# Tiny softmax steps on ScalarE, a second level for product P1, and the sums of the softmax's product on VectorE: a fused attention and ELU kernel on one core

## The chip, the core and the metric

One core of a Trainium2 chip runs the whole kernel. The metric is the device time of one execution in microseconds (us); the time given for a kernel is the median of its runs.

## What is computed

A block-recurrent cross attention is followed by a feed-forward layer with ELU. All data are float32.

```
x: 8 batches, 8 heads, 512 rows, 64;   state: 8, 8, 32, 64
scores  = x @ state^T / 8;   a  = softmax(scores);    xread = a @ state
scores2 = state @ x^T / 8;   a2 = softmax(scores2);   sread = a2 @ x
X = concat(xread, sread) as (4352 rows, 512)       # 544 rows a batch
h = X @ w_in (512 x 2048);   g = h if h > 0 else exp(h) - 1
out = g @ w_out (2048 x 512)
```

Each softmax subtracts its row's maximum and divides by its row's sum plus 1e-9.

## The kernel before

The rows of `xread` (512 a batch) are handled batch by batch; the 32 rows of `sread` of all batches are collected and handled at the end in `states()`. `a @ state @ w_in` is regrouped: for each batch M = state @ w_in is computed (`make_m`), and the first feed-forward product multiplies the softmax `a` (in the buffer `aT`) by M.

Both large products are done by Strassen-Winograd's scheme, in which sums of blocks are formed first and seven products of half size take the place of eight. For the first product the sums of the softmax's blocks are formed by `sum_a` (four subtractions of 128x256 elements), those of M's blocks by `sum_m`, both on GpSimd. For the second product (`ffn2`, class `Strassen`) there are seven products P1 to P7. P2 to P7 are split once more by the same scheme (class `Second`, the "second level"): `weights` forms sums of the weights once, in batch 1, writing one of them over a block of `w_out`; `sums` forms sums of `g` for every batch on VectorE (up to four of 128x512); `steps` gives seven steps, each of four matmuls with 128 columns and one result of 128x128, which VectorE adds to the output buffer `o` from PSUM, or ScalarE copies where the place is fresh. `restore` undoes the overwritten weights for `states()`. P1 (`a11` times `b11`) is not split: 16 matmuls with 256 columns, and one copy of 128x512 by ScalarE.

The softmax of the next batch lies within `ffn2` (`soft_next`): `softmax` for the one that feeds `aT` (transposes, maxima, sums, GpSimd subtracts and multiplies) and `softmax_rows` for the other, which gives `sread`. Three of their steps are tiny `tensor_scalar` instructions on VectorE: the row maximum times minus the scale (128x2), and the 1e-9 added to the sums (128x2 and 128x32).

Nothing is issued in the order in which it is written. Each call records an operation with an estimated cost; `Plan.order` (called at the end) works out due times backwards from TensorE's order and lists the operations engine by engine, GpSimd in the written order. `plan.behind(op)` keeps what is recorded inside it behind the operation `op`; in `soft_next` that is `late[6]`, the last sum of P7's. An operation with `port` set is not planned beside another one that uses the port of VectorE and GpSimd. Since all instructions are issued by one helper, the profile gives them line 464; they are told apart by their buffers: `small` (statistics of the softmax), `xr` (softmax of batches 2 to 7), `s`, `sec` and `m` (sums), `o` (output and next input), `g` (ELU's result), `ps` (PSUM), `w_half` (`make_m`), `xe` (Exp of ELU, and x).

Of the kernel before, what the change touches and what calls it, by code (L numbers as in the profile page):

```python
# [16 lines left out]
AF = mybir.ActivationFunctionType  # L17
ALU = mybir.AluOpType
# [371 lines left out]
def kernel(  # L390
# [21 lines left out]
    scale = 1.0 / math.sqrt(D)  # L412
    eps = 1e-9
# [16 lines left out]
    plan = Plan(psum)  # L430
# [38 lines left out]
    def is_ap(v):  # L469
        return isinstance(v, (View, bass.AP))  # L470

    class Engine:
# [3 lines left out]
        def __getattr__(self, name):  # L476
            def call(**kw):
                outs = [kw[k] for k in ("out", "accum_out") if k in kw]
                ins = [v for k, v in kw.items() if k not in ("out", "accum_out") and is_ap(v)]
                n = max(elements(a) for a in outs + ins) / 1000  # L480
                wide = [a for a in ins if not isinstance(a, View) and elements(a) > 4]
                port = False
                if self.key == DVE:
                    cost = 0.07 + 1.042 * n
                    alone = len(wide) == 1 and not isinstance(kw["out"], View)
                    if alone and name in ("tensor_scalar", "tensor_copy"):
                        cost, port = 0.07 + 0.53 * n, True
                    port = port or len(wide) > 1
                elif self.key == ACT:
                    cost = 0.055 + 0.84 * n  # L490
                    cost += 0.1 * sum(k in kw and is_ap(kw[k]) for k in ("scale", "bias") if k in kw)
                    cost += 0.1 * ("accum_out" in kw)
                else:
                    cost = 0.06 + (1.86 if name == "tensor_tensor" and n > 0.3 else 2.45) * n
                    port = True
                plan.add(
                    self.key, cost, issue(self.engine, name, kw), ins, outs, port,
                    name=name,
                )

            return call

    V, A, Q = Engine(DVE, nc.vector), Engine(ACT, nc.scalar), Engine(POOL, nc.gpsimd)
# [211 lines left out]
    def sum_a():  # L715

        r11, r12, r21, r22 = a_blocks_of(a_sb)
        t1, t2, t4 = (a_sb[:, 1024 + 256 * i : 1280 + 256 * i] for i in range(3))
        (V if 0 else Q).tensor_tensor(out=t1, in0=r12, in1=r11, op=ALU.subtract)
        (V if 0 else Q).tensor_tensor(out=t2, in0=r22, in1=t1, op=ALU.subtract)  # L720
        (V if 0 else Q).tensor_tensor(out=r12, in0=r22, in1=r12, op=ALU.subtract)
        (V if 0 else Q).tensor_tensor(out=t4, in0=r21, in1=t2, op=ALU.subtract)

    def a_blocks_of(a):
        return [a[:, g * 512 + j * 256 : g * 512 + (j + 1) * 256] for g in range(2) for j in range(2)]
# [8 lines left out]
    def read(b, late=False):  # L734
        return kT[:, (b - 1) % (B + 1)] if b != 1 or not late else read_1

    def softmax_rows(b):
        s = st[b, "s"]
        top, total = small(b)[:, 0:2], small(b)[:, 2:4]
        for g in range(G):  # L740
            V.reduce_max(out=tops(b, g)["top"], in_=s[g], axis=AX_X)
        V.tensor_scalar(out=top, in0=top, scalar1=-scale, scalar2=None, op0=ALU.mult)
        for g in range(G):
            A.activation(
                out=soft_a(b, g), in_=s[g], func=AF.Exp, scale=scale, bias=tops(b, g)["top"],
                accum_out=tops(b, g)["total"],
            )
        V.tensor_scalar(out=total, in0=total, scalar1=eps, scalar2=None, op0=ALU.add)
        V.reciprocal(out=total, in_=total)

    def softmax(b, to):
        s = st[b, "s"]
        total_t = small(b)[:, 36:68]

        def rows(g):
            return soft_t(b, g).rearrange("p (k n) -> p k n", n=NS)

        for g in range(G):
            V.transpose(out=soft_t(b, g), in_=s[g])
        for g in range(G):  # L760
            V.reduce_max(out=tops(b, g)["top_t"], in_=rows(g), axis=AX_X)
            (V if 0 & 1 and b > 1 or b in [] else Q).tensor_tensor(
                out=rows(g), in0=rows(g), in1=bc(tops(b, g)["top_t"], NS), op=ALU.subtract
            )
            A.activation(out=soft_t(b, g), in_=soft_t(b, g), func=AF.Exp, scale=scale)
            V.reduce_sum(out=tops(b, g)["total_t"], in_=rows(g), axis=AX_X)
        V.tensor_scalar(out=total_t, in0=total_t, scalar1=eps, scalar2=None, op0=ALU.add)
        V.reciprocal(out=total_t, in_=total_t)
        for g in range(G):
            (V if 0 & 2 and b > 1 or b in [] else Q).tensor_tensor(  # L770
                out=rows(g), in0=rows(g), in1=bc(tops(b, g)["total_t"], NS), op=ALU.mult
            )
            V.transpose(out=to[:, g * 512 : (g + 1) * 512], in_=soft_t(b, g))
# [149 lines left out]
    b11, b12, b21, b22 = (halves(w_k[:, h, :, e]) for e in range(2) for h in range(2))  # L923
# [8 lines left out]
    class Second:  # L932
# [82 lines left out]
    second = {  # L1015
        k: Second(sec[:, i * 1536 : (i + 1) * 1536]) for i, k in enumerate((7, 5, 4, 3, 6))
    }
# [258 lines left out]
    def ffn2(o, b):  # L1276

        c11, c12, c21, c22 = (o.part(i, j) for i in range(2) for j in range(2))
        nxt = b + 1 < B
        spare = spaces(m_sb[:, 1], 3)  # L1280
        o.sum_1()
        late = [plan.ops[-1]]
        if 0:
            second[1].sums(o.a11, spare + s_2[0][:1])
            steps = second[1].steps(c12, fresh=True)
            steps[0]()
        else:
            x1 = o.open()
            o.product(x1, o.a11, b11, True)
            A.copy(out=c12, in_=x1)  # L1290
            steps = []
        if nxt:
            first_m(b + 1, 1)
            scores(b + 1, xr, [f.view() for f in fixed])
        else:
            turn_read()
        for f in steps[1:]:
            f()
        second[2].sums(o.a12, s_2[1] + spaces(a_sb))
        late.append(plan.ops[-1])  # L1300
        for f in second[2].steps(c11, base=c12):
            f()
        late.append(plan.ops[-1])
        second[4].sums(o.a22, s_2[0] + spare[:2])
        late.append(plan.ops[-1])
        for f in second[4].steps(c21, fresh=True):
            f()
        second[6].sums(o.s, s_2[1] + spaces(a_sb))
        late.append(plan.ops[-1])
        combine(o.a12, o.a12, o.s)  # L1310
        late.append(plan.ops[-1])
        steps = second[6].steps(c12)
        second[7].sums(o.a21, s_2[0])
        late.append(plan.ops[-1])
        for f in steps:
            f()
        combine(o.s, o.s, o.a11, ALU.add)
        late.append(plan.ops[-1])

        def soft_next():  # L1320
            if nxt:
                with plan.behind(late[6]):
                    softmax(b + 1, a_sb)
                    softmax_rows(b + 1)
                    load_x(b + 1, x_halves)
                    move_state(b + 1)
                    sum_a()
                    if 1:
                        sum_m(m_to[0])
        if 1==1: soft_next()  # L1330
        V.tensor_tensor(out=c21, in0=c21, in1=c12, op=ALU.add)
        steps = second[7].steps(c22, fresh=True)
        second[5].sums(o.s, s_2[1])
        late.append(plan.ops[-1])
        if 1==2: soft_next()
        for f in steps:
            f()
        V.tensor_tensor(out=c21, in0=c21, in1=c22, op=ALU.add)
        steps = second[5].steps(c12)
        second[3].sums(o.a12, s_2[0])  # L1340
        for f in steps:
            f()
        V.tensor_tensor(out=c22, in0=c22, in1=c12, op=ALU.add)
        store(b, 1, o)
        steps = second[3].steps(c12)
        if nxt:
            make_m(b + 1, 2, 3)
            copy_m(b + 1, 1, m_to[1])
            sum_m(m_to[1])
            state_read(b + 1)  # L1350
        for f in steps:
            f()
        store(b, 0, o)

    def ffn2_1(o, b, x1):
# [36 lines left out]
            f()  # L1392
        store(b, 1, o)
        second[2].weights(b21)
        if 0: second[1].weights(b11)
        for f in second[3].steps(c12):
            f()
        store(b, 0, o)
# [111 lines left out]
    def states():  # L1510
# [7 lines left out]
        for hc in range(5):  # L1518
            fetch_state(hc)
        for k, i in second.items():  # L1520
            if k > 1 or 0: i.restore()
        xT = st["xT"].rearrange("p m b s -> p m (b s)")
        (r11, r12), (r21, r22) = (
            [xT[:, 2 * k : 2 * k + 2, n * P : (n + 1) * P] for n in range(2)] for k in range(2)
# [1 line left out]
        t1, t2, t4 = (  # L1526
            xr[:, 1024 + i * 256 : 1280 + i * 256].rearrange("p (k n) -> p k n", k=2)
            for i in range(3)
        )
# [93 lines left out]
```

## Time and profile before

| | us |
|---|---|
| median of 3 runs (lowest, highest) | 706.02 (704.77, 706.29) |
| the profiled execution | 707.31 |
| its span, first to last instruction | 705.5 |
| TensorE busy | 692.4 |
| VectorE busy | 577.5 |
| ScalarE busy | 301.3 |
| GpSimd busy | 139.4 |

The page divides the span into 40 slices and gives for each the busy tenth of every engine (PE is TensorE, PEld its weight loads, DVE VectorE, ACT ScalarE, POOL GpSimd). A group's line names engine, operation, out<-in and shape, then the count, the busy time in us, the mean of one in ns, and the idle time of the engine ahead of it with what ended it. Instructions of one engine overlap, so a mean is longer than the distance from one start to the next. A matmul of float32 shows as two records.

### The profile page before, as it was taken

The page shows a single profiled execution, that of the slowest core. Times are in us where ns is not written, and L with a number is a line of the kernel's source. Part 1 is how long each engine was busy: PE and PEld are TensorE (multiplying, and loading weights), DVE is VectorE, ACT ScalarE, POOL GpSimd, SP SyncE. Part 2 cuts the span into 40 slices and gives each one's busy share as a digit, 9 for nine tenths or more (in the row PEclk, how much of TensorE's full clock was granted, in tenths as well). Part 3 has the DMA queues.
Part 4 walks back from the last instruction along what each step waited for, and adds up shares of the span by engine and source line. Part 5 has one row for each costly group of instructions (what it writes and reads, how often), then busy time and mean ns, then how long its engine had stood idle before and what let it go on. Part 6 is the DMA issues. An engine that isn't in the chain of part 4 may idle for free.

```text
span 705.5 us, 14564 instructions
## 1 busy us (share of the span) xinstructions
PE 692.4 (98%) x5802; PEld 591.9 (84%) x5802; DVE 577.5 (82%) x1015; ACT 301.3 (43%) x604; POOL 139.4 (20%) x161
## 2 busy tenths in 40 slices
PE   8899999999999999999999999999999999999997
PEld 7544468889988998889888988899888988899996
DVE  3989999999659895899769995989589976997650
ACT  3999982011157123831275125712383127600530
POOL 1310000042121045101630153103520173000000
PEclk9999999999999999999999999999999999999999
DMA  8677773203261406650283316440575026200300
GB/s 193 208 275 256 265 240 58 60 33 118 91 141 70 120 2 181 149 121 1 60 245 77 70 44 189 98 121 1 153 177 120 2 59 212 62 1 31 120 8 23
DMA packets 111268, 78.55 MB, mean 111 GB/s; under 512 B 89184, under 2 KB 92768, under 8 KB 111200
## 3 DMA queue, kind: packets, MB, share of 16 engines
q1 hardware_dynamic: 108988, 77.06, 38.6%
q8 instruction: 46, 0.75, 0.4%
q10 hardware_dynamic: 2212, 0.56, 0.4%
q14 instruction: 22, 0.18, 0.1%
HBM read 61.34 MB, written 13.11 MB: 106 GB/s over the span
## 4 chain that ended last, share of the span: by engine, by line
PE 82%; DVE 12%; DMA 2%; issue 2%; ACT 1%; SPq 1%; ACTq 0%; DVEq 0%
PE ps L464 82%; DVE small L464 3%; DVE o L464 3%; DVE sec L464 2%; DVE s L464 2%; DMA xe<-in_x_dram 1%; DVE g L464 1%; DMA g<-in_x_dram 1%; SPq L464 1%; DVE xr L464 0%; DVE aT L464 0%; PE ps L1581 0%; ACT sec L464 0%; ACT t_w L464 0%; ACTq L464 0%
## 5 line engine op out<-in xcount | busy, mean ns | idle before, releaser
L464 PE MATMUL ps<-aT,m 128*128 128x256 f32 (+1 forms) x568 | 148.8, 406 | 1.1 <-ACT kT L464 1.1
L464 PE MATMUL ps<-w_out,g 128*128 128x128 f32 (+1 forms) x864 | 144.5, 315 | 0.0
L464 PEld LDWEIGHTS ps<-w_out,g 128*128 128x128 f32 x864 | 126.6, 191 | 14.7 <-issue 6.2
L464 PEld LDWEIGHTS ps<-aT,m 128*128 128x128 f32 x568 | 105.1, 190 | 29.1 <-issue 13.1
L464 DVE TENSOR_TENSOR o<-o,ps 128x128 f32<-128x128 f32 (+2 forms) x239 | 66.6, 282 | 50.0 <-PE ps L464 48.5
L464 ACT COPY o<-ps 128x128 f32<-128x128 f32 (+2 forms) x70 | 23.2, 335 | 153.5 <-PE ps L464 153.5
L464 POOL TENSOR_TENSOR xr<-xr,small 128x512 f32<-128x512 f32 x24 | 26.9, 1140 | 306.9 <-PE ps L464 156.9
L464 POOL TENSOR_TENSOR m<-m 128x256 f32<-128x256 f32 x72 | 65.9, 937 | 70.8 <-ACT m L464 69.4
L464 PE MATMUL ps<-sec 128*128 128x128 f32 x560 | 74.0, 275 | 0.0
L464 PEld LDWEIGHTS ps<-sec 128*128 128x128 f32 x560 | 68.4, 192 | 0.4
L464 PE MATMUL ps<-t_w,s 128*128 128x128 f32 (+1 forms) x432 | 65.1, 300 | 3.1 <-DVE o L464 3.1
L464 PEld LDWEIGHTS ps<-t_w,s 128*128 128x128 f32 x432 | 58.4, 191 | 7.3 <-DVE o L464 4.1
L464 ACT ACTIVATE xe<-ps 128x512 f32<-128x512 f32 x96 | 55.5, 600 | 19.5 <-DVE ps L464 12.8
L464 ACT COPY m<-ps 128x512 f32<-128x512 f32 (+1 forms) x56 | 27.1, 535 | 71.8 <-PE ps L464 71.7
L464 ACT COPY sec<-ps 128x512 f32<-128x512 f32 (+1 forms) x52 | 29.8, 574 | 46.0 <-PE ps L464 45.9
L464 DVE SCALAR_TENSOR_TENSOR g<-xe,ps 128x512 f32<-128x512 f32 x66 | 43.7, 679 | 1.2 <-ACT xe L464 1.2
L464 DVE TENSOR_SCALAR xe<-xe 128x512 f32<-128x512 f32 x30 | 15.7, 527 | 31.2 <-ACT xe L464 26.1
L464 PE MATMUL ps<-aT,s 128*128 128x256 f32 x168 | 40.9, 382 | 0.0
L464 ACT ACTIVATE xe<-xe 128x512 f32<-128x512 f32 x66 | 40.0, 637 | 0.9
L464 DVE TENSOR_TENSOR ps<-sec,ps 128x512 f32<-128x512 f32 (+1 forms) x52 | 34.8, 669 | 5.7 <-PE ps L464 4.2
L464 PEld LDWEIGHTS ps<-aT,s 128*128 128x128 f32 x168 | 31.3, 190 | 6.4 <-issue 2.1
L464 PE MATMUL ps<-w_half,kT 64*32 64x256 f32 x1024 | 35.0, 382 | 0.0
(152 smaller groups left out, 1157.4 us busy)
## 6 DMA issues: line engine op xcount, KB each, us to landing
w_half<-w_in_mem SPq DMA_DIRECT2D x54, 512.0 KB
t_w<-in_moe_w_out_dram SPq DMA_DIRECT2D x8, 1024.0 KB
t_w<-in_moe_w_in_dram SPq DMA_DIRECT2D x7, 1024.0 KB
out_dram<-o SPq DMA_DIRECT2D x14, 512.0 KB
xe<-in_x_dram SPq DMA_DIRECT2D x26, 256.0 KB
o<-in_x_dram SPq DMA_DIRECT2D x80, 64.0 KB
w_in_mem<-w_half SPq DMA_DIRECT2D x8, 512.0 KB
xr<-xr SPq DMA_DIRECT2D x96, 32.0 KB
```

The lines of the kernel that those rows point to most:

```text
L464: ins = getattr(engine, name)(**named)
```

## The change

1. The three tiny steps go through a new function `line`, which issues an ACTIVATE with the function Copy on ScalarE for every batch.
2. In batches 2 to 7 P1 is split by the second level too; its weights (of `b11`) are formed in batch 1 and restored in `states()`.
3. `sum_a` runs on VectorE.
4. The softmax of the next batch may start behind `late[3]`, the sums of product 4.
5. The planner takes every `tensor_scalar` of VectorE to use the shared port.

```diff
-                        cost, port = 0.07 + 0.53 * n, True
+                        cost = 0.07 + 0.53 * n
+                    port = name == "tensor_scalar" or alone and name == "tensor_copy"
                     port = port or len(wide) > 1
...
-        (V if 0 else Q).tensor_tensor(out=t1, in0=r12, in1=r11, op=ALU.subtract)
-        (V if 0 else Q).tensor_tensor(out=t2, in0=r22, in1=t1, op=ALU.subtract)
-        (V if 0 else Q).tensor_tensor(out=r12, in0=r22, in1=r12, op=ALU.subtract)
-        (V if 0 else Q).tensor_tensor(out=t4, in0=r21, in1=t2, op=ALU.subtract)
+        (V if 1 else Q).tensor_tensor(out=t1, in0=r12, in1=r11, op=ALU.subtract)
+        (V if 1 else Q).tensor_tensor(out=t2, in0=r22, in1=t1, op=ALU.subtract)
+        (V if 1 else Q).tensor_tensor(out=r12, in0=r22, in1=r12, op=ALU.subtract)
+        (V if 1 else Q).tensor_tensor(out=t4, in0=r21, in1=t2, op=ALU.subtract)
...
+    def line(b, x, a, c):
+        if b >= 0:
+            A.activation(out=x, in_=x, func=AF.Copy, scale=a, bias=c)
+        elif c:
+            V.tensor_scalar(out=x, in0=x, scalar1=c, scalar2=None, op0=ALU.add)
+        else:
+            V.tensor_scalar(out=x, in0=x, scalar1=a, scalar2=None, op0=ALU.mult)
...
-        V.tensor_scalar(out=top, in0=top, scalar1=-scale, scalar2=None, op0=ALU.mult)
+        line(b, top, -scale, 0.0)
...
-        V.tensor_scalar(out=total, in0=total, scalar1=eps, scalar2=None, op0=ALU.add)
+        line(b, total, 1.0, eps)
...
-        V.tensor_scalar(out=total_t, in0=total_t, scalar1=eps, scalar2=None, op0=ALU.add)
+        line(b, total_t, 1.0, eps)
...
-        if 0:
+        if 1:
             second[1].sums(o.a11, spare + s_2[0][:1])
             steps = second[1].steps(c12, fresh=True)
             steps[0]()
...
-                with plan.behind(late[6]):
+                with plan.behind(late[3]):
...
-        if 0: second[1].weights(b11)
+        if 1: second[1].weights(b11)
...
-            if k > 1 or 0: i.restore()
+            if k > 1 or 1: i.restore()
```

## The prediction

> **What bounds the kernel now.** I read the page's busy shares and slices first, then the chain that ended last, then busy time by stretch of one batch, then the timelines of TensorE and VectorE inside that stretch.
>
> ```profile
> PE 692.4 (98%) x5802; PEld 591.9 (84%) x5802; DVE 577.5 (82%) x1015; ACT 301.3 (43%) x604; POOL 139.4 (20%) x161
> ...
> PE   8899999999999999999999999999999999999997
> ...
> DVE  3989999999659895899769995989589976997650
> ACT  3999982011157123831275125712383127600530
> ...
> PE 82%; DVE 12%; DMA 2%; issue 2%; ACT 1%; SPq 1%; ACTq 0%; DVEq 0%
> ```
>
> TensorE is the bound: nine tenths and more in every slice but the first two and the last. ScalarE is at 4 tenths on average, but full in slices 2 to 6 (the start, where weights are converted). The chain leaves TensorE for VectorE in 12% of the span. That part returns every 76.9 us, once in each batch's second product, as the windows of one batch show (columns: window, length, PE, weight loads, DVE, ACT, POOL):
>
> ```profile
> 304.00:319.50 15.50, 15.50 (x160) 13.85 (x159) 13.74 (x24) 3.68 (x8) 0.00 (x0) 1.00 0.59 137
> 319.50:339.20 19.70, 18.93 (x168) 18.55 (x166) 19.68 (x42) 3.92 (x11) 5.14 (x6) 1.00 0.00 1
> 339.20:352.50 13.30, 13.27 (x123) 12.05 (x124) 9.96 (x19) 2.80 (x5) 10.07 (x11) 1.00 0.29 80
> ```
>
> For 19.7 us VectorE has no gap and TensorE loses 0.77 us; before and after it VectorE has 1.76 and 3.34 us free. The loss is at two steps of the second level, which wait for an addition queued on VectorE:
>
> ```profile
> 335.32 1.06 PE L464 MATMUL ps<-sec 128*128 128x128 f32 x8
> 337.00 1.16 PE L464 MATMUL ps<-t_w,s 128*128 128x128 f32 x8 [0.62 <-DVE o L464]
> 338.00 1.06 PE L464 MATMUL ps<-sec 128*128 128x128 f32 x8
> 339.24 1.16 PE L464 MATMUL ps<-sec,s 128*128 128x128 f32 x8 [0.18 <-DVE o L464]
> ```
>
> The same stretches of the batches around it lose 0.62, 0.80, 0.62 and 0.45 us: 3.26 us in five batches. So VectorE is the second bound, by a hair, and only there.
>
> **What the Trainium skill says.** "SBUF — State Buffer", section "Who interferes with whom": VectorE's second port pair is shared with GpSimd as an exclusive lock; `tensor_scalar` can take it, and a VectorE instruction with two SBUF inputs contends with a GpSimd one that reads SBUF. The trace agrees: a `tensor_scalar` on 2 elements takes 625 ns in the mean and up to 1009, where a reciprocal on the same 2 elements takes 145, and the slow ones stand beside GpSimd's `xr` and `aT` work. "ScalarE: Activation LUTs", section "What ACT_TABLE_LOAD costs": an ACTIVATE with immediate scale and bias takes 186 ns + 0.833 ns an element. No such tiny ACTIVATE is in the trace; its smallest ScalarE row, the accumulator read, takes 196 ns, which fits. The same page's rules advise VectorE for an add or a multiply; here the measured 625 ns speaks against that.
>
> ```profile
> L464 POOL TENSOR_TENSOR aT<-aT 128x256 f32<-128x256 f32 x24 | 17.8, 764 | 9.7 <-DVE aT L464 9.7
> ...
> L464 DVE TENSOR_SCALAR small<-small 128x2 f32<-128x2 f32 x12 | 7.5, 625 | 0.0
> ...
> L464 ACT ACTIVATION_READ_ACCUMULATOR xr<-ps,small 128x1 f32 x12 | 2.4, 196 | 0.0
> ...
> L464 DVE RECIPROCAL small<-small 128x2 f32<-128x2 f32 x6 | 0.9, 145 | 0.0
> ```
>
> **The change, part by part.**
>
> *1. P1 by the second level, TensorE.* P1 was 16 matmuls with 256 columns, two records each. An unbroken product of that kind (32 records) starts at 146.07 and its successor at 152.98: 6.91 us. The new P1 is 7 steps of 4 matmuls with 128 columns; such steps of 8 records follow each other at 0.893 us (175.40 to 176.29 below): 7 x 0.893 = 6.25 us. Saved: 0.66 us a batch, six batches (2 to 7): **-4.0 us**. As TensorE has no spare time, this is on the path.
>
> ```profile
> 146.07 7.07 PE L464 MATMUL ps<-t_w,sec 128*128 128x256 f32 x32
> 152.98 7.07 PE L464 MATMUL ps<-w_out,sec 128*128 128x256 f32 x32
> ...
> 175.40 1.06 PE L464 MATMUL ps<-w_out,g 128*128 128x128 f32 x8
> 176.29 1.06 PE L464 MATMUL ps<-t_w,s 128*128 128x128 f32 x8
> ```
>
> *2. What that gives VectorE.* Four sums of 128x512 and three additions of 128x128 from PSUM per batch (the other four results are ScalarE copies: 4 x 265 ns where one copy of 586 stood, on an engine that is idle here). The timeline of VectorE gives start to start:
>
> ```profile
> 310.47 0.28 DVE L464 TENSOR_TENSOR o<-o,ps 128x128 f32<-128x128 f32 x1
> 310.67 0.68 DVE L464 TENSOR_TENSOR m<-g,sec 128x512 f32<-128x512 f32 x1
> 311.27 0.28 DVE L464 TENSOR_TENSOR o<-o,ps 128x128 f32<-128x128 f32 x1
> ```
>
> 0.20 us for an addition, 0.60 for a sum: 4 x 0.60 + 3 x 0.20 = **+3.0 us** of VectorE a batch.
>
> *3. sum_a from GpSimd to VectorE.* Four instructions of 128x256. A VectorE row of that size has a mean of 415 ns where 128x512 has 682; scaled by 0.60/0.68 that is 0.33 us start to start (an estimate): **+1.3 us** of VectorE a batch. GpSimd loses 4 x 764 = 3.1 us. In the new order of instructions these four stand after the last softmax transposes, among the last additions of the batch, so in the stretch with 3.34 us free; the next batch's matmuls that need them come behind `make_m`. Cost on the path: 0. If that cover is gone, 1.3 us a batch.
>
> *4. Tiny steps to ScalarE.* VectorE loses (7.5 + 1.0) / 6 = **1.4 us** a batch (1.0 is the 128x32 row, 6 of 174 ns), all inside the full stretch, and no longer waits there for GpSimd. ScalarE gets three of some 0.19 to 0.21 us (the page's price) where it is 3.92 of 19.70 us busy; one now precedes its own Exp, so a hop between engines goes. Queued behind them on ScalarE are the two Exps and the copies of second-level results; a delay of 0.2 us there is covered by TensorE's alternation between products. On the path: 0.
> In the start it is different: ScalarE is full there, and batches 0 and 1 bring it 6 x 0.2 = 1.2 us, while VectorE, as full, loses four of 431 ns and two of 174: 2.1 us. Bounds: -1.5 to +1.2 us. From 31.8 us on TensorE doesn't wait in the start, and its last wait there (1.07 us) is for ScalarE; I take **+0.3**.
>
> *5. The softmax may start after the sums of product 4 instead of those of product 7.* Nothing is added; VectorE's transposes and maxima move into the stretch before, with GpSimd's `xr` and `m` work behind them (its first four `m` sums no longer stand behind sum_a). Taken at 0, with the range holding both signs.
>
> *6. Weights of the second level for b11, once in batch 1*: 4 sums at 0.68 = 2.7 us of VectorE, in a stage where it is nearly full (5.00 of 5 us in most of 95 to 135) but where TensorE runs on queued work without a gap. In the new order one of the four stands beside the conversions and three among the other weight sums. 0 on the path; at most 2.7. The extra restore at the end (0.6 us) falls where VectorE is idle over half of the time: 0. The planner's port flag changes only the order.
>
> *The stretch together.* VectorE per batch: +3.0 + 1.3 - 1.4 = +2.9 us. From 304.0 to 352.5 it is busy 43.38 of 48.50 us; afterwards 46.3 of 47.84. It still fits, with 1.5 us left instead of 5.1. In the full stretch itself: the 2.4 us of sums come ahead and eat the 1.76 us of gaps, 0.64 late; plus 0.6 of additions, minus 1.4: about -0.2. So the wait stays as it is, some 0.65 us a batch. Sum: -4.0 + 0.3 = -3.7. The profiled execution was 707.31 us (span 705.5 and 1.8 around it), which would become 703.6; it lies 1.3 above the median of 706.02, from which I count: **702.3 us**.
>
> **The rivals.**
> *A, forecast*: P1's gain arrives, the wait stays: 702.3, with 700.5 to 704.8 from the bounds of 4, 5 and a part of 6. Chance 0.60.
> *B, VectorE becomes the bound of the second product.* For it: 19.68 of 19.70 us, and now 97% over 48 us, so any inflation by GpSimd's lock has no room. Against it: sum_a stands where there is room and the port waits go. The place is the stretch 319 to 339; if the tiny steps' 1.4 us doesn't help, because the lock only moves to the next VectorE instruction, the lateness is 0.64 + 0.6 = 1.2 us more a batch and the net 6 x (1.2 - 0.66) = +3.4; with sum_a in the way too, 6 x (2.5 - 0.66) = +11. It decides against the change from 0.66 us of extra wait a batch. I price it at +4: 710. Chance 0.18.
> *C, the waits go as well.* GpSimd's 3.1 us less and no port waits of tiny steps free VectorE by more than 1.4: the 3.26 us of waits vanish too: 706.0 - 4.0 - 3.3 = 698.7. Against it: VectorE's load rises in net. Chance 0.17.
> *D, nothing measurable*: half of the gain eaten by the wait and the rest by the start: 706. Chance 0.05.
>
> **The numbers.** A measurement of this kernel can tell about 0.2% (1.4 us) from no change. Faster by more: A nearly whole, C: 0.75. Within: D and the edge of A: 0.08. Slower: B, less its edge: 0.17. The range reaches from C's time to where B begins to cost: 698.5 to 707.5, leaving out most of B and a little below C.
>
> **What would show it.** Right: P1's steps stand at 0.89 us each in TensorE's timeline, batches recur every 76.2 us instead of 76.9, TensorE's loss in the full stretch stays below 0.8 us, the 128x2 steps show about 0.19 us on ScalarE, and the first `aT` matmuls don't wait for VectorE. Wrong: waits of TensorE for `o`, `m` or `sec` of VectorE over 1.3 us a batch (B), or none (C); a later start of unbroken TensorE work than 31.8 us; a gap between 100 and 170 us (part 6).

## The result, and the profile after

The changed kernel took 702.77 us (median of 19 runs, 701.73 to 705.40) against 706.02 before: the ratio is 0.996, with a 95% interval of 0.9952 to 0.9967, so 3.3 us or 0.46% faster. The forecast was 702.3. The number was met, by luck: two terms of the sum behind it were off, and their errors cancelled. The experiments below show this.

The page of the changed kernel, busy shares, slices of three engines, and the chain by engine:

```profile
PE 689.1 (98%) x5938; PEld 591.8 (84%) x5938; DVE 590.8 (84%) x1062; ACT 307.1 (44%) x646; POOL 121.1 (17%) x137
...
PE   8899999999999999999999999999999999999997
...
DVE  4999999999849996899869995999589977999650
ACT  4998982011058023832176135713283127600530
...
PE 73%; DVE 15%; ACT 5%; DMA 3%; issue 3%; SPq 1%; ACTq 0%; DVEq 0%
```

TensorE executes 136 more records and is busy 3.3 us less. VectorE is busy 13 us more, GpSimd 18 us less. The chain leaves TensorE more often than before, but in other places: it walks mostly through VectorE and ScalarE from 34 to 162.75 us, where TensorE has two waits, of 0.20 and 0.63 us. A chain through an engine is no proof that it holds up another; the waits say that.

TensorE's waits for VectorE's `o` and `g` in the whole span, of before and then of after (columns: waiting engine, buffer, line, what ended the wait, us in total, times, longest):

```profile
PE ps L464 <- DVE o L464: 3.7, 8, 0.6
```

```profile
PE ps L464 <- DVE g L464: 1.3, 2, 0.7
...
PE ps L464 <- DVE o L464: 0.9, 2, 0.6
```

The waits for VectorE's additions to `o` fell from 3.7 to 0.9 us; 1.3 us for `g` are new. The same by batches: I cut both traces at the start of each batch's state read. Before, the four batches 3 to 6 were 76.85, 76.87, 76.45 and 76.40 us long (mean 76.64). After (columns as in the prediction: window, length, PE, weight loads, DVE, ACT, POOL):

```profile
276.94:352.43 75.49, 75.49 (x714) 68.05 (x713) 66.37 (x127) 32.29 (x70) 18.53 (x20) 1.00 0.42 113
352.43:427.85 75.42, 75.42 (x713) 68.23 (x712) 66.22 (x127) 31.98 (x70) 18.36 (x20) 1.00 0.40 106
427.85:504.03 76.18, 75.57 (x713) 68.21 (x713) 66.26 (x127) 32.43 (x70) 18.55 (x20) 1.00 0.38 102
504.03:579.36 75.33, 75.33 (x714) 68.16 (x713) 65.38 (x127) 31.98 (x70) 14.90 (x16) 1.00 0.41 112
```

The mean is 75.61, 1.04 less than before where I had forecast 0.66; only one of the four has a listed wait left (0.61 us).

### The profile page after: what moved, and what is told of

Read it like the earlier page. It is cut to its first block, busy times and chain, and to the rows that moved or that the text cites. A ratio compares the mean times of both kernels' runs of the same rounds, so it can differ in the third digit from the quotient of the medians.

```text
span 700.6 us, 14914 instructions
## 1 busy us (share of the span) xinstructions
PE 689.1 (98%) x5938; PEld 591.8 (84%) x5938; DVE 590.8 (84%) x1062; ACT 307.1 (44%) x646; POOL 121.1 (17%) x137
## 4 chain that ended last, share of the span: by engine, by line
PE 73%; DVE 15%; ACT 5%; DMA 3%; issue 3%; SPq 1%; ACTq 0%; DVEq 0%
PE ps L464 73%; DVE sec L464 3%; DVE g L464 3%; DVE w_out L464 2%; DVE t_w L464 2%; ACT sec L464 2%; DMA t_w<-in_moe_w_out_dram 1%; DVE s L464 1%; DVE w_half L464 1%; DVE xr L464 1%; ACT t_w L464 1%; SPq L464 1%; DMA g<-in_x_dram 1%; DMA xe<-in_x_dram 1%; DVE small L464 1%
## 5 line engine op out<-in xcount | busy, mean ns | idle before, releaser
L464 PE MATMUL ps<-w_out,g 128*128 128x128 f32 (+1 forms) x768 | 113.2, 293 | 0.7 <-DVE g L464 0.7
L464 PEld LDWEIGHTS ps<-w_out,g 128*128 128x128 f32 x768 | 102.5, 192 | 9.1 <-ACT xe L464 2.5
L464 ACT COPY o<-ps 128x128 f32<-128x128 f32 (+2 forms) x88 | 26.1, 300 | 165.2 <-PE ps L464 165.2
L464 DVE TENSOR_TENSOR o<-o,ps 128x128 f32<-128x128 f32 (+2 forms) x257 | 70.9, 286 | 27.7 <-PE ps L464 26.2
L464 POOL TENSOR_TENSOR xr<-xr,small 128x512 f32<-128x512 f32 x24 | 29.3, 1240 | 325.4 <-PE ps L464 173.7
L464 POOL TENSOR_TENSOR m<-m 128x256 f32<-128x256 f32 x72 | 62.8, 894 | 88.2 <-ACT m L464 86.7
L464 DVE TENSOR_SCALAR xe<-xe 128x512 f32<-128x512 f32 x30 | 13.7, 462 | 35.4 <-ACT xe L464 35.3
L464 PE MATMUL ps<-sec,g 128*128 128x128 f32 (+1 forms) x300 | 37.4, 271 | 0.8 <-DMA g<-in_x_dram 0.8
L464 ACT COPY ps<-ps 128x512 f32<-128x512 f32 (+1 forms) x28 | 15.4, 551 | 50.9 <-PE ps L464 50.5
```

Source lines behind the costliest of these rows:

```text
L464: ins = getattr(engine, name)(**named)
```

## The experiments

Theory 1 is the one of the prediction: the matmuls of P1 are the gain, and the tiny steps' relief of VectorE pays for P1's sums. Theory 2: only P1 moves anything. Theory 3: GpSimd's lock on the shared port is what decides. Theory 4: the place of the softmax is. All twelve were timed against the kernel before, whose median in the three groups of runs was 705.79, 705.94 and 705.73 us.

| kernel | P1 split | tiny steps on | sum_a on | us | ratio to before, 95% |
|---|---|---|---|---|---|
| p1_alone | yes | VectorE | GpSimd | 706.37 | 1.0012 (1.0006 to 1.0019) |
| tiny_alone | no | ScalarE | GpSimd | 702.50 | 0.9951 (0.9935 to 0.9967) |
| sum_a_alone | no | VectorE | VectorE | 705.65 | 0.9998 (0.9989 to 1.0007) |
| p1_tiny | yes | ScalarE | GpSimd | 704.83 | 0.9990 (0.9983 to 0.9996) |
| tiny_sum_a | no | ScalarE | VectorE | 702.58 | 0.9951 (0.9939 to 0.9963) |
| p1_tiny_sum_a | yes | ScalarE | VectorE | 703.58 | 0.9965 (0.9954 to 0.9976) |
| tiny_late | no | ScalarE, batches 2 to 7 | GpSimd | 704.98 | 0.9989 (0.9982 to 0.9995) |
| changed, no_p1 | no | ScalarE | VectorE | 704.36 | 0.9984 (0.9973 to 0.9995) |
| changed, tiny_vector | yes | VectorE | VectorE | 707.94 | 1.0044 (1.0028 to 1.0061) |
| changed, tiny_vector_start | yes | ScalarE, batches 2 to 7 | VectorE | 704.88 | 0.9993 (0.9980 to 1.0005) |
| changed, sum_a_pool | yes | ScalarE | GpSimd | 707.16 | 1.0019 (1.0009 to 1.0029) |
| changed, late_6 | yes | ScalarE | VectorE | 703.11 | 0.9957 (0.9940 to 0.9973) |

The first seven have the softmax's place and the planner's port rule of before, the last five those of the change (late_6 has the old place).

How far single executions agree can be read from pairs of traces. p1_tiny_sum_a and late_6 show the same order of instructions on all engines; their medians differ by 0.47 us. The kernel before and sum_a_alone show the same order on TensorE, VectorE, ScalarE and GpSimd up to 150 us, and sum_a_alone is 1.8 us ahead there. So I don't read differences of under 2 us from the starts of two traces. Behind the first cut (182.77 us before, 182.35 after, 182.02 in tiny_alone) the starts play no part: from there to the end it is 522.7 us in the kernel before, 518.3 in the changed kernel and 518.4 in tiny_alone.

**P1 alone.**

```diff
-        if 0:
+        if 1:
             second[1].sums(o.a11, spare + s_2[0][:1])
...
-        if 0: second[1].weights(b11)
+        if 1: second[1].weights(b11)
...
-            if k > 1 or 0: i.restore()
+            if k > 1 or 1: i.restore()
```

> The kernel before with P1 of batches 2 to 7 by the second level and nothing else of the change. Theory 1 (TensorE's 0.66 us a batch is the gain, and it is only kept because the tiny steps leave VectorE): without their 1.4 us of relief VectorE falls 1.2 us a batch further behind, so 706.0 + 3.4, about 709, and TensorE's waits in the stretch grow from 0.65 to about 1.9 us a batch. Theory 2 (VectorE's gaps take the 3.0 us of new sums and additions by themselves): about 702, waits as before.

It was 0.12% slower than before, near neither number. P1's larger matmuls are gone and nearly all of the saving is taken back: behind the first cut the trace is 1.2 us shorter than before's (521.5 us), and its start 1.3 us longer. Theory 2 falls; theory 1 has the sign and a fifth of the size (+0.6 us for +3.4), but not by the way it named: TensorE's listed waits in batches 3 to 6 did not grow to 1.9 us a batch, they are 0.4 (0.7 before).

**The changed kernel without P1** (the same three lines, back).

> The changed kernel with P1 undivided again (16 matmuls of 256 columns), all else changed. Theory 1: VectorE loses 1.4 us of tiny steps in the stretch and gets sum_a where it has room, so the waits of 0.65 us a batch go: about 703. Theory 2 (P1 is the whole gain, the rest moves nothing): 706. If P1's matmuls save 4.0 us and nothing else matters the difference to the changed kernel is 4.0 us; if only the waits had gone, it is 0.

704.4, between the two. P1 is worth 1.6 us in this company, not 4.0. Even that is no gain over the best kernel without P1: tiny_sum_a, which differs from no_p1 by the softmax's place and the planner's port rule alone, took 702.58, so without P1 those two cost 1.8 us.

**The tiny steps back on VectorE in the changed kernel.**

```diff
-        if b >= 0:
+        if b >= 99:
             A.activation(out=x, in_=x, func=AF.Copy, scale=a, bias=c)
```

> The changed kernel with the tiny steps back on VectorE in all batches. Theory 1: VectorE gets its 1.4 us a batch back in a stretch that has no gap, of which some 1.2 us become waits of TensorE in batches 2 to 6, so 702.8 + 6, about 709. Theory 2: VectorE still has room and the time stays within 1.4 us of 702.8.

5.2 us slower than the changed kernel, near the 6 of theory 1, but by another way. The group of the 128x2 steps in this kernel, whose planner keeps every `tensor_scalar` apart from GpSimd's work:

```profile
L464 DVE TENSOR_SCALAR small<-small 128x2 f32<-128x2 f32 x12 | 2.2, 183 | 0.0
```

The instruction itself now takes 183 ns, where it took 625 before. The time is lost all the same: batches of 76.4 us instead of 75.6, and a start that is 3.9 us longer. So the cost is not only what the tiny step waits for the port. That keeping it apart shifts other work in the order is my reading; no run holds the order fixed.

**Tiny steps on ScalarE alone, on the kernel before.** The edit is `line` and its three calls, as in the diff of the change.

> The kernel before with the tiny steps of all batches on ScalarE and nothing else. Theory 1: 1.4 us less in a stretch without gaps, so the waits of 0.65 us in five batches go: about 703. Theory 2 (nothing but P1 matters): 706.

702.50: theory 1's number, and the whole gain of the change by itself. The four batches of this kernel:

```profile
277.42:353.06 75.64, 75.64 (x690) 67.77 (x689) 62.03 (x116) 32.05 (x67) 21.04 (x25) 1.00 0.41 103
353.06:428.69 75.63, 75.63 (x689) 67.76 (x688) 62.03 (x116) 32.06 (x67) 21.02 (x25) 1.00 0.41 108
428.69:504.33 75.64, 75.64 (x689) 67.76 (x688) 62.05 (x116) 32.06 (x67) 21.04 (x25) 1.00 0.39 102
504.33:579.97 75.64, 75.64 (x689) 67.76 (x688) 62.03 (x116) 32.06 (x67) 19.65 (x23) 1.00 0.40 106
```

TensorE does the same work as before and never waits: 75.64 us. That is 1.00 less than before, where the idle time that the trace lists was only 0.71 a batch in the mean. VectorE's busy time falls from 65.04 a batch (mean of the four) to 62.04: 3.0 us, twice the 1.4 that I had counted for the instructions moved. The rest is in other instructions beside GpSimd: of the VectorE sums of 128x512 without a PSUM operand, the 32 in these batches that overlap a GpSimd instruction take 1050 ns in the mean before and 879 in tiny_alone; the 76 that overlap none take 681 and 685. The tiny steps themselves, in this kernel on ScalarE:

```profile
402.23 0.19 ACT L464 ACTIVATE small<-small 128x2 f32<-128x2 f32 x1
402.45 0.69 ACT L464 ACTIVATE xr<-ps,small 128x512 f32<-128x512 f32 x1
403.03 0.19 ACT L464 ACTIVATION_READ_ACCUMULATOR xr<-ps,small 128x1 f32 x1
...
403.93 0.20 ACT L464 ACTIVATE small<-small 128x2 f32<-128x2 f32 x1
407.81 0.23 ACT L464 ACTIVATE small<-small 128x32 f32<-128x32 f32 x1 [2.42 <-DVE small L464]
```

0.19 to 0.23 us each, on an engine with room.

**P1 and the tiny steps**, without the other three parts.

> The kernel before with P1 by the second level and the tiny steps on ScalarE, but sum_a on GpSimd, the softmax behind the sums of product 7 and the planner's old port rule. Theory 1 (these two are the change, the rest is neutral): 702 to 704. A theory in which the earlier softmax or sum_a on VectorE is what makes room: 706 or above.

704.83, outside theory 1's interval and short of the other's 706: added to the tiny steps, P1's second level costs 2.3 us. The two are not the whole of the change.

**The changed kernel with sum_a on GpSimd** (`V if 1` to `V if 0` in its four lines).

> The changed kernel with sum_a on GpSimd as before. Theory 1: sum_a lay in VectorE's free stretch, so taking it away gives nothing there; GpSimd's 3.1 us come back ahead of the m sums. 702.8 within 1. Theory 3 (GpSimd's lock is what costs VectorE its time): 3.1 us more of GpSimd's work beside VectorE makes it slower, 704 to 706.

707.16: 4.4 us slower than the changed kernel, and theory 1's number was wrong. The sign is that of theory 3, and the trace bears it out for a part. Batches 2 to 6 together grew from 397.0 to 399.8 us, 0.55 us each, and TensorE's listed waits for VectorE's `g` in batches 3 to 6 from 0.6 to 1.8. VectorE lost 2.4 us of sum_a a batch, but its busy time fell by only 0.4, because other instructions grew beside GpSimd: `g<-g` of 128x512 from 716 to 928 ns in the mean. The rest can't come from sum_a's own run on GpSimd: the start up to the first step of the second level grew from 158.4 to 163.3 us, and its first sum_a begins at 157.7 us, when nearly all of that is past. Its waits of TensorE before 163 us, and those of the changed kernel before 158:

```profile
PE ps L464 <- ACT m L464: 3.6, 3, 3.0
```

```profile
PE ps L464 <- ACT m L464: 0.6, 2, 0.4
```

ScalarE's order differs from 47 us on, long ahead of the first sum_a: the planner, given another cost late in the program, chose another order for the start. How much of the 4.9 us lies in that order and how much in the variation from run to run (this trace is of a run of 709.6 us, 2.4 above the kernel's median) one trace can't say.

**The changed kernel with the softmax's old place** (`late[3]` to `late[6]`).

> The changed kernel with the softmax behind the sums of product 7 as before. Theory 1: neutral, 702.8 within 1. Theory 4 (the earlier softmax spreads VectorE's work over the gaps, and that is where the waits went): the waits of 0.6 us a batch and more return, 706 or above.

703.11: no difference to the changed kernel that can be told. Batches 3 to 6 are 75.65 us. Theory 4 falls for the changed kernel. As this kernel and p1_tiny_sum_a have one order, the planner's port rule changed nothing here.

**The changed kernel with the tiny steps of batches 0 and 1 on VectorE** (`b >= 0` to `b >= 2`).

> The changed kernel with the tiny steps of batches 0 and 1 alone on VectorE. In the profile after, the start up to the first step of the second level is 1.5 us shorter than before. If the tiny steps do that (VectorE full in the start), it comes back: 704. By my prediction (ScalarE full, +0.3 for the change): 702.5.

704.88. The batches are the same as in the changed kernel (75.63) and the start is 162.3 us instead of 158.4. My +0.3 for the start had the wrong sign in this pair. Against tiny_vector, whose start is as long (162.3), it also divides the 5.2 us: 2.1 for batches 0 and 1, 3.1 for batches 2 to 7.

**Tiny steps on ScalarE from batch 2 on, on the kernel before** (`line` with `b >= 2`).

> The kernel before with the tiny steps of batches 2 to 7 alone on ScalarE. The start then keeps its order of before (159.9 us up to the first second-level step), and only the batches change: from 76.6 to 75.6 us each as with all tiny steps moved. If the batches carry the gain of the tiny steps: 706 - 5 = 701 to 702 with the start left as it was, 0 to 1 us off the 702.5 of all eight. If the start carries a third of it (1.4 us): 703.9.

704.98, 1.1 us beyond the worse of the two expectations. Its batches of 76.14 us give half of tiny_alone's gain, though both kernels do the same work in them; VectorE is busy 62.51 us a batch in it and 62.04 in tiny_alone. In each of the four TensorE waits once more for an addition to `o` (0.17 us listed; the starts of the two steps around it, 344.70 and 345.99, are 1.29 us apart instead of 0.89). Those four batches are 2.0 us of the difference; their edit is the same, so the other order makes it. Its start (158.8) is as short as tiny_alone's, so in this pair the start doesn't account for the difference.

```profile
344.70 1.12 PE L464 MATMUL ps<-w_out,g 128*128 128x128 f32 x8
345.99 1.16 PE L464 MATMUL ps<-sec 128*128 128x128 f32 x8 [0.17 <-DVE o L464]
```

**sum_a on VectorE alone, and with the tiny steps.**

> The kernel before with sum_a on VectorE and nothing else. Theory 1: it falls where VectorE has room and takes 3.1 us from GpSimd: 706 within 1. If VectorE's load in the stretch decides: up to 1.3 us a batch slower, 712. If GpSimd's lock decides: 704 or less.

> The kernel before with the tiny steps on ScalarE and sum_a on VectorE, P1 undivided. With the tiny steps alone TensorE's waits in batches 3 to 6 are gone and 702.5 is reached; sum_a then has nothing to give, 702.5 within 1. If sum_a on VectorE is what P1's second level is in need of and costs by itself, 703 to 704.

705.65 and 702.58: nothing in either company, as theory 1 expected.

**P1, tiny steps and sum_a.**

> The changed kernel but for the softmax's place and the planner's port rule. P1 with the tiny steps alone is 704.8, the changed kernel 702.8. If sum_a on VectorE makes the difference: 702.8 within 1. If it is the port rule and the earlier softmax: 704.8.

703.58, between the two numbers, within the 1 us of the first. With P1, sum_a on VectorE gives 1.3 us (704.83 to 703.58); without P1 it gave nothing.

## Why the prediction was right, and where it wasn't

*The result (702.3 forecast, 702.77 measured)*: right in size and sign; of the steps, two were off in opposite directions.

*Part 1, P1's matmuls, -0.66 us a batch*: the steps cost what was forecast, but not the batch. Where neither kernel has a listed wait, a batch with P1 split is at best 75.33 us (the changed kernel's last window above; the other two are 75.42 and 75.49) and one without is 75.64 (tiny_alone): **0.31** at most, half of the forecast. In the order of TensorE one sees the other half. First tiny_alone, then the changed kernel, around `make_m` (`w_half`) and the scores (`xr,kT`); 64*32 in a line means that the matmuls use a part of TensorE's array of that size (small tiles), 128*128 that they use all of it:

```profile
376.20 4.48 PE L464 MATMUL ps<-w_out,g 128*128 128x256 f32 x20
380.61 1.09 PE L464 MATMUL ps<-w_half,kT 64*32 64x256 f32 x32
381.50 1.06 PE L464 MATMUL ps<-xr,kT 64*32 64x512 f32 x16
382.49 2.05 PE L464 MATMUL ps<-w_out,g 128*128 128x128 f32 x16
384.38 1.06 PE L464 MATMUL ps<-t_w,g 128*128 128x128 f32 x8
```

```profile
370.32 1.89 PE L464 MATMUL ps<-aT,m 128*128 128x256 f32 x8
372.05 1.05 PE L464 MATMUL ps<-w_out,g 128*128 128x128 f32 x8
373.03 1.09 PE L464 MATMUL ps<-w_half,kT 64*32 64x256 f32 x32
374.06 1.99 PE L464 MATMUL ps<-aT,m 128*128 128x256 f32 x8
375.89 1.05 PE L464 MATMUL ps<-w_out,g 128*128 128x128 f32 x8
376.78 1.06 PE L464 MATMUL ps<-t_w,g 128*128 128x128 f32 x8
377.67 1.06 PE L464 MATMUL ps<-w_out,g 128*128 128x128 f32 x8
378.66 1.09 PE L464 MATMUL ps<-xr,kT 64*32 64x512 f32 x16
379.68 1.16 PE L464 MATMUL ps<-w_out,g 128*128 128x128 f32 x8
380.67 1.06 PE L464 MATMUL ps<-sec,m 128*128 128x128 f32 x8
```

Without P1's steps these two products of small tiles stand side by side, and `make_m` takes 0.89 us to the next start. With them, the planner puts full-size matmuls between: `make_m` takes 1.03, the eight records ahead of it 0.98 instead of 0.89, and the eight behind it 1.83 instead of the 1.73 of the eight at 370.32. "TensorEngine Tiling (Array Packing)" of the Trainium skill, section "Key Properties", says that a change of the tiling mode drains TensorE; the trace agrees, at about 0.1 us at each end of such a group. From start to start, less the full-size records at 0.893 for eight of 128 columns and 1.73 for eight of 256, the two groups cost 2.07 us side by side (376.20 to 384.38) and 1.22 + 1.21 apart (372.05 to 375.89 and 377.67 to 380.67): 0.36 us more, which is the whole of the missing 0.35. In batches 3 to 6 TensorE enters small tiles five times a batch in tiny_alone and six times in the changed kernel. No run splits P1 and keeps the two groups together, so this is worked out from the traces and not tested.
The mis-sized term was not P1's own steps but what they are put between.

*Parts 2 and 3, VectorE's load*: +3.0 and +1.3 us forecast; the changed kernel has 66.06 us a batch (mean of the four) and tiny_alone 62.04: +4.0. Right in sum. sum_a is dearer than assumed: the first three of its four instructions start 0.86 us apart in one batch (422.29 to 424.02), partly beside GpSimd's `s` sums and with an addition between. The 24 take 579 ns in the mean: those beside an `s` sum 656 to 916, the others 409 to 430. It lies where VectorE has room, as forecast, and sum_a_alone shows that this costs nothing.

*Part 4, the tiny steps, -1.4 us of VectorE a batch and the wait of TensorE unchanged in the sum*: this failed. The relief is 3.0 us, because other VectorE instructions shrink too, as shown under tiny_alone; and the wait that it ends is 1.00 us a batch, not 0.65. The lines shown in the prediction had the larger number: the steps at 335.32, 337.00, 338.00 and 339.24 are 1.68, 1.00 and 1.24 us apart, 3.92 us for three steps that take 0.893 each unhindered: 1.24 lost where the trace lists 0.62 + 0.18 of idle. I had read the idle time in brackets and not the distance.
So the expected equal wait became a gain of about 0.7 us a batch against the smaller gain of P1.

*Part 4 in the start, +0.3*: wrong in sign by the pair tiny_vector_start and changed kernel (2.1 us in the medians). The edit changes the planner's order there as well, so the runs don't tell the instructions' own cost from the order's; and tiny_late, whose start has its tiny steps on VectorE like the kernel before, is as short there as tiny_alone.

*Part 5, the softmax's place, 0*: right beside P1 (late_6); without P1 the place and the port rule together cost 1.8 us (no_p1 against tiny_sum_a). *Part 6, weights and restore, at most 2.7*: not separated, but small. From the first step of the second level to the first cut it took 23.97 us after and 22.88 before, with one new wait of 0.63; p1_alone, which has the new weights too, took 23.08 without a wait, and tiny_alone, which hasn't, 23.52; the last stage took 121.2 and 120.9 though P1 of batch 7 is in it, so part of P1's gain is given back there. The cause of that stays open.

*The signs*: P1's steps do stand 0.89 us apart, and the tiny steps take 0.19 to 0.23 us on ScalarE. But batches recur every 75.6 us and not 76.2, and three of the four have no listed wait, which had been named as a sign of C. TensorE's last wait in the start is at 45.40 us (0.20 us) instead of 31.80, which had been named as a sign of being wrong; the start is no longer for it (158.4 us against 159.9).

*The rivals*: C's mechanism happened (the waits went) and A's didn't hold as written; C's price failed because it left P1 its full 4.0. B's loss, not its size, is seen where the tiny steps stay on VectorE: p1_alone, where P1's gain is used up, and tiny_vector, at +0.4%.

What is shown: the tiny steps alone, with the order that the planner makes of them, give the whole result; P1's split changes the time by between -1.6 and +2.3 us, by what it is combined with (1.6 gained in the changed kernel, against a no_p1 that is itself 1.8 behind tiny_sum_a; 0.6, 1.0 and 2.3 lost in the three pairs with the old port rule, of which the smallest is hardly more than the 0.5 by which one order differed from itself); sum_a on VectorE helps only beside P1. What is not shown: how much of each such difference is the instructions and how much the planner's new order. tiny_late against tiny_alone puts 2.5 us on an edit that leaves the work of batches 2 to 7 alone. Whether the tiny steps pay by leaving the port, or by the order, would need a run with the order held. No version beat the changed kernel by more than can be told: tiny_alone is 702.50 with a third of the edits.

## What to carry to other kernels

Take the cost of a wait on a pipelined engine from the distance of the starts against the undisturbed distance, not from the idle time listed. Where a planner writes the order, test each part of a change alone before adding savings up: the parts here are -3.4, +0.6 and -0.1 us by themselves, and -3.3 together. Look first for the tiny instruction in the full stretch of the second-busiest engine; here moving it was worth more than a cheaper product on the busiest one.

## What was not expected of the hardware

- A wait of TensorE cost more than its listed idle time: 0.80 us listed, 1.24 lost in three steps, as above; in tiny_late 0.17 listed and 0.50 lost a batch against tiny_alone.
- A group of small-tile matmuls made the full-array records ahead of it and behind it about 0.1 us longer each; cut off from its neighbour, one group cost 0.36 us more, half of the saving of 0.66.
- A `tensor_scalar` on 2 elements took 625 ns in the mean (146 to 1009) in the order of before and 183 ns where the planner kept it apart from GpSimd; the ACTIVATE in its place 197 to 200 ns.
- A VectorE subtraction of two 128x256 inputs took 409 to 430 ns by itself and 656 to 916 beside a GpSimd one.
